# Input blocks asked for in held-back groups, fewer tables ahead of the loop, and folds at other chunks

## The chip, the cores and the metric

The kernel runs on one core of a Trainium2 chip. The metric is the device time of one execution in microseconds; a kernel's time is the median of its timed runs. One further execution is profiled, and all rows of the trace come from that one.

## What is computed

Eight sequences `x` of 6336 rows by 128 channels are convolved along the rows, channel by channel, with a filter `h` of the same length (written with Fourier transforms of twice the length). Then, for each sequence, the 128 rows with the largest scores `y @ w_gate` go through a two-layer perceptron, and its result, weighted by the sigmoid of the score, is added to them.

```
Xf = rfft(x, n=2*S, axis=1);  Hf = rfft(h, n=2*S, axis=0)
y = irfft(Xf * Hf, n=2*S, axis=1)[:, :S]
for b in range(B):
    s = y[b] @ w_gate;  top = the 128 rows of largest s
    y[b, top] += sigmoid(s[top])[:, None] * (relu(y[b, top] @ w1) @ w2)
```

## The kernel before, in words

The transform is done in two steps of matrix products, on 50 x 128 points. Work goes in **units**: unit -1 is the filter `h`, units 0 to 7 hold the input. Each unit has eight input **blocks** of 512 KB, numbered through: blocks 0 to 7 are `h`, 8 to 15 unit 0, 16 to 23 unit 1. `load_x` (L122 to L129) asks SyncE's queue for a block; `place` (L114) gives its room: the blocks up to 15 share nine rooms in turn, so that block 9 reuses block 0's room, and so on.

A block is first **folded** (`fold`, L131): an addition (L134) and a subtraction (L135) of its two halves, by VectorE or GpSimd. **Stage A** (`products_a`, L196) multiplies it with a table (`fah` for the filter, `fa` for the input), in two half-blocks t = 0 and 1 of 32 matrix instructions each. The results lie in one of three PSUM places in turn, and `leave_a` evicts them to `reg` (L211 on VectorE, L213 on ScalarE). For the filter and the first three blocks of unit 0 ScalarE evicts alone; from block 11 on VectorE takes a part or every third half-block.

Behind stage A of units -1 and 0 stands the **loop** over 13 chunks c of four frequencies ("j" in the plan): `stage_h` multiplies the filter's chunk by a table `wbuf` (L110; ScalarE L245 and L246, VectorE L253, and the spectrum is written out to `hd`), `stage_b` does the same with unit 0's chunk, VectorE multiplies it with the spectrum (L284), and GpSimd joins the parts (two operations at L289 per chunk). In the loop the blocks 16 to 23 of unit 1 are asked for, one per chunk from chunk 0 on (two there), and folded. Stage A of block 16 stands ahead of the last chunk, that of 17 to 23 behind it. Then stage C of unit 0 (L302) begins, which reads what GpSimd joined.

The program is one list of steps (`plan`), and each engine executes its part in the order in which the steps write it. What sets the order around the change:

- Before the first step the blocks 0 to 8 are asked for. Behind the second half-block of block m (m from 0 to 6) block m + 9 is asked for; it waits until TensorE has read block m.
- `fold_to(n)` emits all folds up to block n: in stage A of units -1 and 0 four blocks ahead, all on VectorE; blocks 16 to 20 and 22 on GpSimd, 21 and 23 on VectorE. In the loop it is called at chunk 0 (blocks 16, 17), and behind chunks 3, 6 and 9 (18, 19, 20); blocks 21 to 23 follow behind the last chunk.
- `ask` requests the tables of the next users, as far as six rooms reach. Behind the first half-block of blocks 9, 11 and 13 ScalarE copies one column into the next table's room (L855), and two tables are asked for; since they write the same room, SyncE can't issue them before ScalarE has written the column, and ScalarE writes it behind the evictions ahead of it. So six tables are there for the loop.
- SyncE issues its transfers in order: one that waits holds all behind it.

Of the kernel before, what the change touches and what calls it, by code (L numbers as in the profile page):

```python
# [33 lines left out]
def conv_moe(ctx, tc, x, h, w_gate, w1, w2, fa_d, wb_d, wc_d, at_d, tri_d, cst_d, outs):  # L34
    nc = tc.nc
    v = nc.vector
    g = nc.gpsimd
# [54 lines left out]
    edges = cp.tile([128, 2], F32, name="edges")  # L92
# [19 lines left out]
    blocks = {}  # L112
# [9 lines left out]
    def load_x(n):  # L122
        u, q = n // 8 - 1, n % 8
        t = place(n)
        for i in range(2 if n == 0 else 1):
            w = slice(i * 512, i * 512 + 512) if n == 0 else slice(0, 1024)
            nc.sync.dma_start(out=t[:, w], in_=h[q, :, w] if u < 0 else x[u, q])
        blocks[n] = (t[:, 0:1024].rearrange("p (d s m) -> p d s m", d=8, s=2),
                     t[:, 1024:1536].rearrange("p (d m) -> p d m", d=8))  # L129

    def fold(n, eng):  # L131
        for i in range(2 if n == 0 else 1):
            xs, es = [a[:, i * 4:i * 4 + 4] if n == 0 else a for a in blocks[n]]
            eng.tensor_tensor(out=es, in0=xs[:, :, 0], in1=xs[:, :, 1], op=ALU.add)  # L134
            eng.tensor_tensor(out=xs[:, :, 0], in0=xs[:, :, 0], in1=xs[:, :, 1], op=ALU.subtract)  # L135
# [611 lines left out]
    for u in range(NU):  # L747
        if u + 2 <= NU:
            both = merge(c_list(u), b_list(u + 1))
            n = next(i for i, s in enumerate(both) if s[0] == "b") + 2 * (u % 2)  # L750
# [17 lines left out]
    def ask(used, most=len(users)):  # L768
        while asked[0] < most:
            s = users[asked[0]]  # L770
            if s[0] == "d" and s[1] + 1 == NU:
                break
            own = [o for o in users[used:asked[0] + 1] if o[0] == "b" and o[1] >= SINGLE and o[2] % 2]
            if len(own) > 2 or s in own and s[1] > last_a[0]:
                break
            if sum(1 if o[0] == "j" else 0 if o in own else 3 if o[0] == "b" and o[1] >= SINGLE else 2
                   for o in users[used:asked[0] + 1]) > 6:
                break
            tabs[s] = (load_d if s[0] == "d" else load_b)(*s[1:])
            asked[0] += 1  # L780
# [23 lines left out]
            next(others[0], None)  # L804

    nc.sync.dma_start(out=fah, in_=fa_d[:, 1])
    for n in range(9):
        load_x(n)
    v.memset(ones16, 1.0)
    v.memset(edges[:, 0:1], -1.0)  # L810
# [2 lines left out]
    done = [1]  # L813

    def fold_to(n):
        while done[0] <= min(n, 23):
            fold(done[0], v if done[0] < 16 or done[0] in (21, 23) else g)
            done[0] += 1

    def load_constants():  # L820
# [8 lines left out]
    for s in plan:  # L829
        kind, unit = s[0], s[1]  # L830
        n = (unit + 1) * 8
        delay[0] = kind == "c" and unit + 1 == NU and not later_half and s[2] != 15
        share[0] = 5 if kind in "bc" and unit + 1 < NU or kind == "b" or delay[0] else 7
        if kind in "bdj":
            ask(used)
            used += 1
        if kind == "a":
            q, t = s[2:]
            if unit < 2 and t == 0 and (unit < 1 or q):
                fold_to(min(n + q + 4, 15) if unit < 1 else 23)  # L840
            if unit >= 2 and (q, t) == (3, 0):
                fold(n + 7, g)
            stage_a(*s[1:])
            if (q, t) == (7, 1):
                last_a[0] = unit
            if unit + 1 == NU and (q, t) == (1, 0):
                fold(n + 6, g)
            if t and n + q < 7:
                load_x(n + q + 9)
            if t and (unit, q) == (-1, 3):  # L850
                nc.sync.dma_start(out=cst, in_=cst_d)
                nc.sync.dma_start(out=fa, in_=fa_d[:, 0])
            if not t and unit == 0 and q in (1, 3, 5):
                at = used_room[0] * 512
                nc.scalar.copy(out=wbuf[:, at:at + 1], in_=edges[:, 0:1])  # L855
                ask(0, q + 1)
            if unit >= 2 and (q, t) == (1, 0):
                load_x(n + 7)
            if t:
                visit("pqx" if q in (2, 4, 7) else "x")  # L860
        elif kind == "j":
            c = s[2]
            if c == 0:
                load_x(16)
                load_x(17)
                spectra.append(stage_h(0, tabs[s][0])())
            join = stage_h(c + 1, tabs["j", -1, c + 1][0]) if c + 1 < len(KCH) else None
            n = KCH[c][1] * HD
            st = spectra.pop()
            early = c + 2 == len(KCH)  # L870
            if early:
                spectra.append(join())
            if c == 0:
                fold_to(17)
            stage_b(0, c, (tabs.pop(s)[0], [st[:, 0:n], st[:, n:2 * n]]))
            if join and not early:
                spectra.append(join())
            if 0 < c < 7:
                load_x(17 + c)
            if c == 2:  # L880
                load_constants()
            if c in (3, 6, 9):
                fold_to(17 + c // 3)
        elif kind == "b":
            stage_b(*s[1:], tabs.pop(s))
            if (unit, s[2]) == (1, 1):
                v.tensor_copy(out=upper16[0:LN], in_=upper)
                v.tensor_copy(out=ident16, in_=ident)
                v.tensor_copy(out=lanes16[:, 0:1], in_=cst[:, 0:1])
                v.tensor_scalar(out=lanes16[:, 1:2], in0=cst[:, 0:1], scalar1=-1.0, scalar2=None, op0=ALU.mult)  # L890
            if unit == SINGLE and s[2] in (9, 11):
                load_x((unit + 2) * 8 + s[2] // 2 + 1)
            visit("pqx" if s[2] % 2 or s[2] == 12 else "x")
        elif kind == "c":
            stage_c(*s[1:])
            i = HALVES.index(s[2] // 2 * 2)
            free = True
            if unit + 2 < NU and s[2] % 2:
                m = (unit + 3) * 8
                last = unit + 3 == NU  # L900
                for q in ((0,), () if last else (5,), (1,) if last else (6, 1), (4,), (2, 3), (), (), ())[i]:
                    load_x(m + q)
                q = (None, 0, None, None, 1, 4, 2, (3, 5))[i] if last else (None, 0, 5, 6, 1, 4, 2, 3)[i]
                free = i < 6
                for q in (q if isinstance(q, tuple) else () if q is None else (q,)):
                    fold(m + q, g if free or q == 5 else v)
            if unit + 1 == NU:
                for k in range(2):
                    if loaded[0] < 1:
                        load_w(loaded[0])  # L910
                        loaded[0] += 1
                if s[2] not in (4, 12):
                    visit("pq", False)
                    visit("vlx")
                if not later_half:
                    if count[0] < 4:
                        fetch()
                else:
                    if s[2] not in (0, 2, 8, 11):
                        more()  # L920
                    if s[2]:
                        visit(of=(strands,))
            else:
                visit(("vlx" if free else "x") if s[2] % 2 else "x")
        elif kind == "d":
            busy[0] = unit + 1 == NU
            stage_d(*s[1:], tabs.pop(s))
            i = s[2]
            if unit + 2 < NU:
                visit("x" if i % 2 or i == 6 else "vlx")  # L930
            elif unit + 1 == NU:
                hold[0] = i > 0
                visit(of=(strands, others) if i == 4 else None)
        elif kind == "end":
            if unit >= SINGLE:
                strands.append(search([unit], False))
                if unit + 1 == NU:
                    visit(of=(strands,))
            flush()
            busy[0] = False  # L940
            if unit == SINGLE:
                later_half.append(1)
                serial[0] = True
                while loaded[0] < 6:
                    load_w(loaded[0])
                    loaded[0] += 1
                others.append(experts())
                for i in range(8):
                    tabs["d", NU - 1, i] = load_d(NU - 1, i)
            if unit < SINGLE and unit % 2:  # L950
                strands.append(search([unit - 1, unit], True))
                if len(strands) == 1:
                    visit("x", False)
# [104 lines left out]
```

## Time and profile before

| | us |
|---|---|
| median of 3 timed runs | 779.13 |
| lowest and highest | 778.33, 780.61 |
| the profiled execution | 785.05 |
| its span, first to last instruction | 783.3 |
| TensorE busy in the span | 732.8 |
| VectorE, GpSimd, ScalarE busy | 628.5, 552.6, 450.3 |

The profiled execution is 5.92 us longer than the median of the timed ones, and its time lies 1.75 us above its span. Stage A of units -1 and 0 ends at 42.37 us of the span, the loop's last chunk and stage A of unit 1 lie between about 85 and 103 us. In a row of the trace, PE is TensorE's matrix products, PEld its weight loads, DVE VectorE, ACT ScalarE, POOL GpSimd, SPq SyncE's queue; L196 is line 196 of the kernel; "<-" behind an idle time names what ended it, and "issue" is time in which an engine waited for nothing that the profile shows.

### The profile page before, as it was taken

Reading aid. Unit: us, or ns where it says so; the run is one execution under the profiler, and the core shown is the slowest. Engines: PE = TensorE matmul, PEld = TensorE weight load, DVE = VectorE, ACT = ScalarE, POOL = GpSimd, SP = SyncE. Lnnn points to the kernel's source line nnn. Section 1 sums busy time; section 2 is a strip of 40 time slices with the busy share of each in tenths; the row PEclk is TensorE's granted clock in tenths of the full one; section 3 lists DMA queues with packets and bytes.
Section 4 is the critical chain, followed back from the end, with each engine's and each line's share of the span. In section 5 each row is a group of like instructions: output and inputs, shape, how many; then the busy total and the mean of one; then the engine's idle time right before and its main releaser. Section 6 shows DMA issues by size and latency. Waiting matters only on the chain.

```text
span 783.3 us, 39717 instructions
## 1 busy us (share of the span) xinstructions
PE 732.8 (94%) x17566; PEld 630.7 (81%) x17566; DVE 628.5 (80%) x1072; ACT 450.3 (57%) x966; POOL 552.6 (71%) x407
## 2 busy tenths in 40 slices
PE   6799999999999999999999999999999998879585
PEld 6766778888889888888898879878898888868475
DVE  6579956866676799999877999998878988965982
ACT  5687744465346566666365566655565666655561
POOL 0058939976997599859967798768995667533743
PEclk9999999999999999999999999999999999999879
DMA  8559547477856775678557765799579636541400
GB/s 325 174 196 335 207 144 252 147 212 238 278 162 208 236 260 190 184 232 270 191 170 231 261 215 162 207 349 306 167 205 319 212 106 183 146 162 30 151 12 14
DMA packets 82292, 157.64 MB, mean 201 GB/s; under 512 B 9366, under 2 KB 30088, under 8 KB 82120
## 3 DMA queue, kind: packets, MB, share of 16 engines
q1 hardware_dynamic: 81224, 154.05, 61.1%
q8 instruction: 138, 2.26, 1.2%
q0 software_dynamic: 896, 1.05, 0.5%
q14 instruction: 34, 0.28, 0.1%
HBM read 121.77 MB, written 33.29 MB: 198 GB/s over the span
## 4 chain that ended last, share of the span: by engine, by line
PE 70%; DVE 15%; issue 5%; DMA 4%; POOL 2%; SPq 1%; ACT 1%; POOLq 0%; DVEq 0%; ACTq 0%
PE pb L302 23%; PE pt L110 20%; PE pb L322 11%; PE pt L196 10%; PE pb L110 3%; PE pm L110 2%; DVE cmp L476 2%; DVE reg L278 2%; DVE tx L278 2%; DVE ss L354 1%; PE pb L196 1%; DVE st L331 1%; DVE st L332 1%; DVE num L478 1%; DMA big<-tab_wb 1%
## 5 line engine op out<-in xcount | busy, mean ns | idle before, releaser
L303 ACT COPY half<-pb 114x512 f32<-114x512 f32 x224 | 147.3, 657 | 165.3 <-PE pb L302 159.4
L338 POOL TENSOR_TENSOR tm<-st,wg 114x1024 f32<-114x1024 f32 x56 | 134.0, 2395 | 53.6 <-DVE st L332 36.4
L289 POOL TENSOR_TENSOR reg<-reg,tx 128x512 f32<-128x512 f32 (+1 forms) x104 | 130.9, 1293 | 43.5 <-PE pb L302 17.7
L289 POOL TENSOR_TENSOR big<-big,tx 128x512 f32<-128x512 f32 (+1 forms) x104 | 132.3, 1303 | 24.3 <-DVE tx L284 13.9
L302 PE MATMUL pb<-wc,reg 128*50 128x64 f32 x4096 | 125.6, 219 | 5.2 <-issue 3.5
L302 PEld LDWEIGHTS pb<-wc,reg 128*50 128x50 f32 x4096 | 120.3, 126 | 10.0 <-issue 5.6
L302 PE MATMUL pb<-wc,big 128*50 128x64 f32 x4096 | 120.7, 219 | 0.8 <-ACT reg L213 0.5
L302 PEld LDWEIGHTS pb<-wc,big 128*50 128x50 f32 x4096 | 118.4, 126 | 3.2 <-ACT reg L213 0.7
L322 PE MATMUL pb<-half,wbuf 114*50 114x128 f32 x1792 | 110.6, 273 | 2.0 <-ACT half L303 0.7
L322 PEld LDWEIGHTS pb<-half,wbuf 114*50 114x50 f32 x1792 | 96.2, 122 | 8.6 <-issue 1.3
L110 PE MATMUL pt<-big,wbuf 128*64 128x256 f32 x704 | 85.9, 388 | 0.0
L110 PE MATMUL pt<-reg,wbuf 128*64 128x256 f32 x704 | 84.9, 388 | 0.1
L284 DVE TENSOR_TENSOR tx<-pt,wbuf 128x1024 f32<-128x1024 f32 (+1 forms) x65 | 76.4, 1175 | 0.0
L213 ACT COPY reg<-pt 128x800 f32<-128x800 f32 x63 | 55.7, 936 | 33.1 <-PE pt L196 32.8
L110 PEld LDWEIGHTS pt<-big,wbuf 128*64 128x64 f32 x704 | 50.7, 135 | 23.8
L110 PEld LDWEIGHTS pt<-reg,wbuf 128*64 128x64 f32 x704 | 50.7, 135 | 22.6 <-issue 0.2
L331 DVE TENSOR_TENSOR st<-pb,st 114x512 f32<-114x512 f32 x56 | 38.6, 689 | 36.0 <-PE pb L322 22.6
L356 DVE TENSOR_REDUCE ss<-tm 114x16 f32<-114x1024 f32 x48 | 58.4, 1217 | 7.6 <-POOL tm L338 6.9
L213 ACT COPY big<-pt 128x800 f32<-128x800 f32 x56 | 49.4, 935 | 22.6 <-PE pt L196 22.5
L284 DVE TENSOR_TENSOR reg<-pt,wbuf 128x1024 f32<-128x1024 f32 (+1 forms) x39 | 45.9, 1176 | 16.6 <-PE pt L110 16.6
L196 PE MATMUL pt<-fa,big 50*64 50x100 f32 x2304 | 58.7, 249 | 0.3 <-issue 0.3
L196 PEld LDWEIGHTS pt<-fa,big 50*64 50x64 f32 x2304 | 51.3, 133 | 6.7 <-issue 4.0
(182 smaller groups left out, 1211.9 us busy)
## 6 DMA issues: line engine op xcount, KB each, us to landing
wbuf<-tab_at SPq DMA_DIRECT2D x112, 200.0 KB
out<-st SPq DMA_DIRECT2D x112, 200.0 KB
wbuf<-tab_wb SPq DMA_DIRECT2D x84, 256.0 KB
wbuf<-hd SPq DMA_DIRECT2D x84, 256.0 KB
big<-in_x SPq DMA_DIRECT2D x37, 512.0 KB
half<-in_x SPq DMA_DIRECT2D x15, 512.0 KB
hd<-st SPq DMA_DIRECT2D x24, 256.0 KB
reg<-in_x SPq DMA_DIRECT2D x12, 512.0 KB
```

Of the source, the lines that this page charges most:

```text
L110: nc.tensor.matmul(out[lo:hi], w[:, lo:hi], r, **k)
L196: nc.tensor.matmul(o, w, tab[lanes, c], start=True, stop=True)
L213: nc.scalar.copy(out=o, in_=i)
L278: v.tensor_tensor(out=o, in0=src[:, b], in1=f, op=ALU.mult)
L284: v.tensor_tensor(out=dst.rearrange("p h a j k t -> p k h a j t"), in0=src, in1=w, op=ALU.mult)
L289: g.tensor_tensor(out=yv[:, :, r], in0=yv[:, :, r], in1=zv[:, :, 1 - r], op=ALU.add if r else ALU.subtract)
L302: nc.tensor.matmul(pt[i2 * 64:i2 * 64 + N1, o:o + HD], w, wc[:, i2], start=True, stop=True)
L303: nc.scalar.copy(out=hv[0:LN, c * 4 + j:c * 4 + j + 2].rearrange("p j r m t -> p (j r) t m"), in_=pt[0:LN].rearrange("p (j t m) -> p j t m ...
L322: nc.tensor.matmul(pt[r][a * 64:a * 64 + N1, c * 128:c * 128 + 128], ats[c // 2][0:LN, c % 2, a, r], hv[0:LN, :, r, m], start=True, stop=True)
L331: v.tensor_tensor(out=st[:, 0:512], in0=pt[1][0:LN], in1=st[:, 512:1024], op=ALU.add)
L338: (v if split else g).tensor_tensor(out=tm.rearrange("p (a d) -> p a d", d=n), in0=st.rearrange("p (a d) -> p a d", d=n), in1=w.unsqueeze( ...
L356: v.tensor_reduce(out=ss[u][:, :, :, 4 * i:4 * i + 4].rearrange("p b s c -> p s c b"), in_=tm.rearrange("p (s c b d) -> p s c b d", s=2, c ...
```

## The change

Blocks 0 to 5 are asked for ahead of the first step, in place of 0 to 8. The others are asked for in four groups, each behind the first half-block of an earlier block: 6 to 8 behind block 3, 9 to 11 behind block 5, 12 and 13 behind block 7, 14 and 15 behind block 9. Ahead of each group ScalarE writes a column of its first block's room. The folds on VectorE go up to the last block asked for, and three in place of four blocks ahead in unit 0. The tables ahead of the loop are four in place of six: the column and two tables behind block 11, and the same behind block 13; the next two are asked for at the loop's first chunk, ahead of blocks 16 and 17. In the loop GpSimd folds blocks 18, 19 and 20 behind chunks 2, 4 and 6, and block 22 behind chunk 9; blocks 21 and 23 are folded by VectorE behind the last chunk, as before.

```diff
     nc.sync.dma_start(out=fah, in_=fa_d[:, 1])
-    for n in range(9):
+    for n in range(6):
         load_x(n)
...
     def fold_to(n):
         while done[0] <= min(n, 23):
-            fold(done[0], v if done[0] < 16 or done[0] in (21, 23) else g)
+            if done[0] != 22:
+                fold(done[0], g if 15 < done[0] < 21 else v)
             done[0] += 1
...
             if unit < 2 and t == 0 and (unit < 1 or q):
-                fold_to(min(n + q + 4, 15) if unit < 1 else 23)
+                fold_to(min(n + q + (4 if unit < 0 else 3), max(blocks), 15) if unit < 1 else 23)
...
-            if t and n + q < 7:
-                load_x(n + q + 9)
+            group = {3: (6, 9), 5: (9, 12), 7: (12, 14), 9: (14, 16)}.get(n + q, ())
+            if group and not t:
+                nc.scalar.copy(out=place(group[0])[:, 0:1], in_=edges[:, 0:1])
+                for m in range(*group):
+                    load_x(m)
             if t and (unit, q) == (-1, 3):
                 nc.sync.dma_start(out=cst, in_=cst_d)
                 nc.sync.dma_start(out=fa, in_=fa_d[:, 0])
-            if not t and unit == 0 and q in (1, 3, 5):
+            if not t and unit == 0 and q in (3, 5):
                 at = used_room[0] * 512
                 nc.scalar.copy(out=wbuf[:, at:at + 1], in_=edges[:, 0:1])
-                ask(0, q + 1)
+                ask(0, q - 1)
...
-            if c in (3, 6, 9):
-                fold_to(17 + c // 3)
+            if c in (2, 4, 6):
+                fold_to(17 + c // 2)
+            if c == 9:
+                fold(22, g)
```

## Rows read from the trace of the kernel before

**Rows 1.** Page: an engine's busy us, share, instructions; a queue's packets, MB, share.

```profile
PE 732.8 (94%) x17566; PEld 630.7 (81%) x17566; DVE 628.5 (80%) x1072; ACT 450.3 (57%) x966; POOL 552.6 (71%) x407
...
q8 instruction: 138, 2.26, 1.2%
```

**Rows 2.** Chain of waits, 18 to 48 us: start us, us, what.

```profile
19.12 2.29 issue
...
40.11 1.00 issue
...
42.37 2.87 PE pb L110 x24
```

**Rows 3.** Busy time by stretch: window, us, engines with records, PEclk, DMA share, GB/s.

```profile
15.90:18.87 2.97, 2.97 (x138) 2.97 (x132) 2.90 (x6) 2.69 (x5) 0.00 (x0) 1.00 1.06 412
18.87:21.41 2.54, 0.25 (x12) 0.11 (x5) 2.33 (x5) 0.94 (x2) 0.00 (x0) 1.00 0.98 358
21.41:25.21 3.80, 3.80 (x125) 3.80 (x127) 3.49 (x7) 3.06 (x5) 0.00 (x0) 0.70 0.76 270
25.21:29.90 4.69, 3.57 (x135) 3.37 (x129) 2.99 (x5) 3.84 (x7) 0.00 (x0) 0.88 0.41 126
29.90:33.58 3.68, 3.15 (x127) 3.03 (x126) 0.47 (x1) 3.09 (x6) 0.00 (x0) 1.00 0.30 77
...
37.10:41.11 4.01, 3.01 (x129) 2.89 (x128) 2.14 (x3) 1.93 (x5) 0.00 (x0) 1.00 0.57 165
...
93.28:96.91 3.63, 3.05 (x138) 2.85 (x127) 3.60 (x3) 3.63 (x8) 3.63 (x4) 1.00 0.04 11
96.91:100.57 3.66, 3.03 (x126) 2.84 (x128) 1.96 (x4) 1.80 (x4) 2.43 (x2) 1.00 0.02 4
```

**Rows 4.** DMA queues in the window 18.8 to 20.0 us.

```profile
q8 instruction: 1, 0.02, 5.6%
```

**Rows 5.** ScalarE's timeline; then SyncE's waits to 140 us (total, times, longest).

```profile
16.50 1.73 ACT L213 COPY reg<-pt 128x800 f32<-128x800 f32 x2 [0.28 <-PE pt L196]
...
31.28 0.18 ACT L855 COPY wbuf<-edges 128x1 f32<-128x1 f32 x1
...
SPq L157 <- ACT wbuf L855: 11.2, 3, 6.4
```

**Rows 6.** Timelines of VectorE and of SyncE's queue in stage A.

```profile
8.18 0.69 DVE L134 TENSOR_TENSOR half<-half 128x512 f32<-128x512 f32 x1 [2.47 <-DMA half<-in_h]
...
22.60 0.33 SPq L127 DMA_DIRECT2D half<-in_x  x1
...
24.67 0.33 SPq L127 DMA_DIRECT2D half<-in_x  x1
...
26.18 0.69 DVE L134 TENSOR_TENSOR half<-half 128x512 f32<-128x512 f32 x1 [0.28 <-DMA half<-in_x]
...
28.88 0.69 DVE L134 TENSOR_TENSOR half<-half 128x512 f32<-128x512 f32 x1 [1.21 <-DMA half<-in_x]
...
35.63 0.99 DVE L211 COPY big<-pt 128x800 f32<-128x800 f32 x1
```

**Rows 7.** GpSimd's timeline in the loop.

```profile
50.53 2.51 POOL L289 TENSOR_TENSOR big<-big,tx 128x512 f32<-128x512 f32 x2 [1.06 <-DVE tx L284]
...
61.47 2.52 POOL L289 TENSOR_TENSOR big<-big,tx 128x512 f32<-128x512 f32 x2 [1.15 <-DVE tx L284]
...
85.87 1.29 POOL L134 TENSOR_TENSOR half<-half 128x512 f32<-128x512 f32 x1
```

**Rows 8.** Busy time by stretch inside the loop, columns as in rows 3.

```profile
80.00:85.00 5.00, 5.00 (x48) 3.45 (x46) 4.79 (x7) 3.76 (x8) 4.11 (x5) 1.00 0.85 293
```

**Rows 9.** Timelines of GpSimd and TensorE behind the loop.

```profile
96.33 1.73 POOL L134 TENSOR_TENSOR half<-half 128x512 f32<-128x512 f32 x1
...
98.60 0.25 PE L196 MATMUL pt<-fa,half 50*64 50x100 f32 x1
99.47 1.57 PE L196 MATMUL pt<-fa,half 50*64 50x100 f32 x59 [0.62 <-POOL half L135]
```

## The prediction

> **What bounds the kernel now.** The page first: TensorE is busy for 94% of the span [rows 1], so a gain elsewhere counts only where TensorE stands still. The change touches only the stretch from the start to the end of the table loop and the stage A behind it, some 100 of 783 us. So the second view is the chain of waits in that stretch. After block 1 (folded from 8.18 us on [rows 6]) TensorE runs without a named wait up to the loop at 42.37, but with five pieces called "issue", the first of 2.29 us, the last of 1.00 [rows 2].
>
> What are these? TensorE executes 2 x 17566 instructions, and the queue named "instruction" moved 138 packets of together 2.26 MB [rows 1]: 35132/138 = 255 instructions and 16.4 KB each, a page. Cut at the five gaps, with cuts put between them by counting, each stretch of stage A holds 252 to 270 instruction records of both TensorE columns, those over a cut counted twice: every gap lies at the end of a page [rows 3]. The page needed at 18.87 is asked for when its forerunner begins, at 15.90; its packet shows up only in the window 18.8 to 20.0 [rows 4], with the DMA engines full (shares 1.06 and 0.98 [rows 3]), and TensorE goes on at 21.41.
>
> So stage A is **paced by the fetch of its own instructions**. From one page to the next it takes 3.63 and 3.66 us when the DMA engines are idle (share 0.04, 0.02), 3.68 and 4.01 us at shares of 0.30 and 0.57, and 5.51 us (15.90 to 21.41) when they are full; between lies 25.21 to 29.90, 4.69 us, with two single blocks in flight [rows 3]. The work of a page takes 2.97 us (15.90 to 18.87), and ScalarE's two evictions per block 0.9 us each [rows 5], 3.6 per page of two blocks. After an idle 2.5 us the granted clock is also lower for a while (0.70, 0.88), between its two levels, 1.2 and 2.4 GHz [rows 3].
>
> The Trainium skill (Runtime: NRT & Kernel Launch, section Instruction fetch mechanics) says the same of the size, 16 KiB pages of 256 instructions, but calls their cost mostly hidden; this trace differs, with up to 2.54 us at one page.
>
> **The change part by part.** The profiled execution took 785.05 us, its span 783.3; the median of the timed runs is 779.13 (778.33 to 780.61). I work out differences in the profiled execution and put them, unchanged in us, on the median. About 0.3%, 2.3 us, is what a measurement of this kernel can tell from no change.
>
> *Blocks 6 to 8 held back.* Before, nine blocks were asked for at once and land in line, one per 1.27 us (512 KB at 412 GB/s [rows 3]). Block 1 stood behind block 0's two halves only, so I take its landing as unchanged, and TensorE's work up to 15.9 us with it; a shorter queue could not help it by more than one block's 1.27 us. By the line, block 5 is there at 8.18 + 4 x 1.27 = 13.3 us. The first ScalarE column stands behind the eviction of block 3's first half, 16.50 + 0.88 [rows 5], and takes 0.18 [rows 5], so block 6 is asked for at 17.6. A block asked for with little ahead of it was folded 3.6 us (22.60 to 26.18) and 4.2 us (24.67 to 28.88) later [rows 6]: block 6 can be folded at 21.2 to 21.8, block 7 1.3 us later, block 8 another 1.3.
>
> *The same delay helps one page.* At 15.90 the DMA engines now have been idle since 13.3, so the page arrives after 3.6 us, at 19.5, in place of 21.41: 1.9 us ahead. Half of that is lost at once, since block 6's first fold (0.69 [rows 6]) ends at 21.9 to 22.5 and TensorE, done with block 5 at about 20.5 (some 1.0 us of work behind the page), waits for it; before, it came to block 6 at 22.4. Block 7 can start at 23.4 (its fold follows block 6's two operations), and the page boundary in its second half is reached at 24.2 in place of 25.21: 1.0 us ahead.
>
> *Blocks 9 to 15.* Their groups are released by the evictions of blocks 5, 7 and 9: 17.6 + 4 x 0.92 = 21.3, then about 25.7 and 29.4. So the queue is full nearly without a break until block 15 lands at about 34 to 35; before, the share fell to 0.76 and 0.41 from 21.4 us on [rows 3]. The next pages are now fetched against it. I take 5.0 us for the page from 24.2 (between 4.69 and 5.51), 4.4 for the next (between 3.68 and 4.69: the last group is still in line), 3.75 for the third (two tables only) and 4.2 for the fourth (four tables and blocks 16 and 17 in one burst; 4.01 before, with two tables and those two blocks): 29.2, 33.6, 37.35, 41.55. Before: 29.90, 33.58, 37.10, 41.11. **The lead of 1.9 us is given back page by page, and stage A ends 0.45 us later.** Bounds: all four pages at 3.6 would end at 38.6, **-2.5 us**; a start at 24.9 and 5.5, 4.7, 4.0, 4.7 would end at 43.8, **+2.7**.
>
> *What is queued behind the new waits.* SyncE stands behind each column, with cst and fa behind block 8: fa's 100 KB take 0.25 us at that rate, and block 8's first fold, 0.69 us, hides them. VectorE's folds of 14 and 15 now stand ahead of the evictions it shares from block 11 on; block 15's fold began at 28.88 and ended 1.5 us later; now it ends at about 36.5. Its eviction of block 12's first half (35.63, 0.99 us [rows 6]) moves to about 37.5; TensorE wants that bank again at block 13's second half, about 37.8 by the pages above. Covered, barely; priced in the upper bound. The columns add 4 x 0.19 and one held table column is gone: 0.6 us of ScalarE, which is idle for 0.6 to 2.1 us of each page from 21.41 on [rows 3]: nothing.
>
> *The clock.* If TensorE's waits at 20.4 and 19.1 lower it again, the page costs what that from 21.41 to 25.21 cost, 3.80 us without a gap at 0.70 [rows 3], which is less than a fetch against a full queue; inside the bounds.
>
> *Four tables in place of six, 16 and 17 behind them.* The loop needs two tables at its start, asked for at about 34.5, eight us ahead of it: hidden. Blocks 16 and 17 come some 1.3 us later; GpSimd folds them ahead of its first join, where it was idle for 1.06 us [rows 7]; the rest of the delay falls into the 1.15 us that each later chunk leaves. Cost 0.
>
> *Folds behind chunks 2, 4, 6 and 9.* GpSimd's pair of joins takes 2.52 of a chunk's 3.6 us, with 1.15 us idle; a fold takes two operations of 1.29 [rows 7]. After 2, 4 and 6 its joins run up to 2.0 us late, caught up by chunk 9, since three folds take 7.7 us and seven chunks leave 8. The slot behind chunk 9 (85.87) holds block 22's fold in place of block 20's. TensorE in the loop is busy 5.00 of every 5 us and hides it all [rows 8]. What goes is the fold of 22 behind the last join (from 96.33), for which TensorE stood still between its starts at 98.60 and 99.47, **0.87 us** [rows 9]. But the pages are late next: 93.28, 96.91, 100.57, 3.63 and 3.66 apart with the DMA engines idle [rows 3]. Without the wait, TensorE reaches the end of that page at 99.7 and stands until 100.57. **I take 0**; bounds -0.87 and 0 (above 0 needs a late GpSimd, whose joins are done by 96.33, while TensorE comes to their reader behind stage A only).
>
> Sum: +0.45 + 0 = +0.45 us; 785.5 for a profiled execution, **779.6** for the median.
>
> **Rivals.**
> *Quiet fetch, faster.* If groups of two and three leave the fetches room, all pages take 3.6: -2.5, with block 1 unchanged, 776.6. For it: the gap of 2.29 goes in any case. Against it: two single blocks already made 4.69. If the fetch cost nothing, the data and ScalarE would bound: from block 6's fold at 22.0, ten half-blocks at 0.92 and three columns end at 32.5, the ten that VectorE shares at 2.97/4 each at 39.9, against 42.37: -2.4, and with the 0.87 behind the loop -3.3: 775.8. That would be the outcome by the skill's rule (Runtime: NRT & Kernel Launch, Instruction fetch mechanics). The middle of both: **776.2**.
> *Late loads, slower.* The mechanism is the queue kept full from 18 to 35 us: each page is fetched against it, and block 15's fold, held ahead of evictions on VectorE, comes due together with the burst of four tables and two blocks. It decides from an average of 4.8 us per page on; price +2.7: **781.8**. For it: 5.51 us is on record for a full queue. Against: the last two pages meet lighter traffic.
> *The change doesn't hold.* Should the column not hold the load back, the order is much as before and the time 779.1; but such columns ahead of the tables made SyncE wait 11.2 us on ScalarE [rows 5], so they do hold.
>
> **How the numbers follow.** Forecast (a stage A within +-2.3 us) 0.60, columns that don't hold 0.02, quiet fetch 0.22, late loads 0.16. The quiet rival is over the 0.3% line at its middle, the late one too: faster 0.22, same 0.62, slower 0.16. The range reaches to the bounds, -2.5 and 0.6 of -0.87 below, +2.7 above: 776.1 to 782.0.
>
> **What would show it.** Right: the gap near 19 us falls under 1 us; TensorE waits for block 6 with about 1 us; the gaps at the next pages' ends grow to 1.5 to 2.5 us, named "issue", with the instruction packets starting 2 us or more after the page began; the loop's first product starts at 42 to 43; no wait for a GpSimd fold near 99, but an "issue" gap of 0.7 to 0.9 before 100.6. Wrong: pages of 3.6 us under a full queue, block 1 earlier than 7.5 us, or VectorE's folds of 14 and 15 named as what TensorE waited for.

## The result

| | before | changed |
|---|---|---|
| median of 14 runs, us | 779.13 | 783.86 |
| lowest and highest, us | 777.08, 781.38 | 778.44, 787.86 |
| the profiled execution, us | 785.05 | 782.47 |
| its span, us | 783.3 | 780.7 |

The ratio is 1.0053 [1.0034, 1.0073]: **the change costs 4.1 us (2.6 to 5.7)**, and the medians differ by 4.7; that is more than the 2.3 us that a measurement can tell from no change. The forecast, 779.6 and "same", was wrong; the time lies above its range (its sum gives 781.8 at the top, not 782.0; both are below), on the side of the rival called late loads.

The two profiled executions lie the other way round than the medians, before's 5.9 us above its own, the changed one's 1.4 below. The whole spans therefore can't be compared; the stretch from the start to stage C of unit 0 can. First the page of the changed kernel, beside [rows 1]:

```profile
span 780.7 us, 39723 instructions
PE 728.5 (93%) x17566; PEld 636.3 (81%) x17566; DVE 628.5 (81%) x1072; ACT 449.6 (58%) x969; POOL 551.9 (71%) x407
```

The instructions are the same but for ScalarE's, 969 in place of 966 (four columns more, one table column fewer): no work was added that could take 4 us. Next stage A cut at the ends of its instruction pages, with the columns of [rows 3], and two pages behind the loop:

```profile
14.55:17.68 3.13, 3.13 (x136) 2.91 (x128) 0.11 (x1) 3.13 (x8) 0.00 (x0) 1.00 0.19 39
17.68:23.88 6.20, 3.55 (x137) 2.99 (x127) 3.07 (x5) 4.13 (x8) 0.00 (x0) 1.00 1.02 369
23.88:28.13 4.25, 3.45 (x128) 3.03 (x127) 3.76 (x7) 3.50 (x8) 0.00 (x0) 1.00 0.85 327
28.13:32.39 4.26, 3.18 (x128) 3.02 (x127) 3.46 (x6) 3.39 (x6) 0.00 (x0) 1.00 0.76 238
32.39:37.83 5.44, 3.20 (x126) 2.82 (x126) 4.11 (x7) 2.29 (x4) 0.00 (x0) 0.93 0.67 208
37.83:43.07 5.24, 5.24 (x128) 5.24 (x131) 2.24 (x4) 1.75 (x4) 0.00 (x0) 0.50 0.49 149
43.07:44.70 1.63, 1.63 (x59) 1.50 (x52) 0.91 (x2) 0.25 (x1) 0.00 (x0) 0.73 1.07 227
...
95.77:99.41 3.64, 3.06 (x131) 2.86 (x128) 3.49 (x3) 3.64 (x8) 2.98 (x3) 1.00 0.03 10
99.41:103.33 3.92, 3.03 (x126) 2.83 (x127) 1.95 (x3) 2.37 (x4) 0.00 (x0) 1.00 0.02 4
```

The reader is to see three things. The page that ends at 17.68 ended at 21.41 before [rows 3], so the first gap named "issue" is gone and TensorE is **3.73 us ahead**: 1.35 us because this page began at 14.55 and not at 15.90, 2.38 because of the gap. The page behind it takes 6.20 us against full DMA engines (share 1.02) and hands most of that back: 23.88 stands against 25.21. TensorE stands still in it nearly as long as it did in the gap of 2.29 us, now for block 6 (start us, us, engine, line, operation, with the idle time before it and what ended it):

```profile
20.69 0.35 PE L196 MATMUL pt<-half 50*64 50x100 f32 x2 [1.92 <-DVE half L134]
```

And the last two pages take 5.44 and 5.24 us, the second of them at a granted clock of 0.50, the lower of its two levels, where before it took 4.01 at full clock [rows 3]: 43.07 stands against 41.11. The loop's first product starts at 44.77 in place of 42.37 [rows 2], **2.40 us late**, and stage C of unit 0 at 105.83 in place of 103.03: nothing was made up on the way. Stage C's line in the chain of the kernel before:

```profile
103.03 3.79 PE pb L302 x128
```

The chain of waits says what TensorE stood for (start us, us, what):

```profile
19.85 0.70 DVE half L134
...
23.43 0.45 issue
...
29.51 0.21 ACT half L851
...
29.74 4.23 DMA half<-in_x
...
34.09 0.70 DVE half L134
...
35.49 0.58 DVE big L211
...
36.68 1.15 issue
...
44.77 2.87 PE pb L110 x24
...
102.44 0.89 issue
...
105.83 3.81 PE pb L302 x128
```

Block 6's fold (19.85) stands in the chain where the first gap was. In the page from 32.39 the chain comes from the held load: ScalarE's column at 29.51, block 14 landed 4.23 us later, its fold at 34.09, an eviction on VectorE at 35.49 behind it, for which TensorE stands still for 1.09 us (35.03 to 36.12). But what ends last in that page is again a gap at its end, 1.15 us. The DMA queues in a few windows of this trace (packets, MB, share of the 16 engines) show what the gaps are. From 17.7 to 21.2 us the queue "instruction" shows no packet, and in the next window one:

```profile
q1 hardware_dynamic: 347, 1.29, 100.8%
...
q1 hardware_dynamic: 356, 0.39, 115.1%
q8 instruction: 1, 0.02, 5.2%
...
q8 instruction: 1, 0.02, 8.3%
```

The first line is 17.7 to 21.2, the next two 21.2 to 22.3, the last 100.4 to 101.4. The page begun at 17.68 asks for its follower, and that follower's packet starts 3.5 to 4.6 us later; in 32.4 to 35.3 there is none either, and one in 35.3 to 36.5. With a quiet queue it starts within 1.0 to 1.3 us: in the page begun at 99.41 nothing moves until 100.4, and the one packet of 100.4 to 101.4 starts at 100.7.

### The profile page after: what moved, and what is told of

Read it like the earlier page. It is cut to its first block, busy times and chain, and to the rows that moved or that the text cites. A ratio compares the mean times of both kernels' runs of the same rounds, so it can differ in the third digit from the quotient of the medians.

```text
span 780.7 us, 39723 instructions
## 1 busy us (share of the span) xinstructions
PE 728.5 (93%) x17566; PEld 636.3 (81%) x17566; DVE 628.5 (81%) x1072; ACT 449.6 (58%) x969; POOL 551.9 (71%) x407
## 4 chain that ended last, share of the span: by engine, by line
PE 67%; DVE 17%; DMA 6%; issue 4%; ACT 3%; SPq 1%; POOL 1%; POOLq 0%; DVEq 0%; ACTq 0%
PE pb L302 22%; PE pt L110 19%; PE pb L322 11%; PE pt L196 10%; PE pb L110 3%; DVE cmp L476 2%; DMA out<-st 2%; PE pm L110 2%; DVE tx L278 2%; DVE reg L278 2%; PE pb L196 1%; DVE ss L354 1%; DVE st L331 1%; DVE st L332 1%; ACT junk L487 1%
## 5 line engine op out<-in xcount | busy, mean ns | idle before, releaser
L110 PEld LDWEIGHTS pt<-big,wbuf 128*64 128x64 f32 x704 | 58.5, 135 | 16.6
```

The costliest lines, as they stand in the source:

```text
L110: nc.tensor.matmul(out[lo:hi], w[:, lo:hi], r, **k)
```

## Experiments

Two theories stood at the start. **Late loads on VectorE** (theory A, later L, in the expectations): blocks 14 and 15 are asked for so late that their folds hold VectorE's evictions, and TensorE waits for a PSUM place. **Fetches against bursts** (D, later F): a group of blocks issued at once stands in front of the fetch of the next instruction page; TensorE stands still, and its clock is lower behind that. Theories B and C put the loss on the tables and on the loop's folds.

### Parts of the change alone

Each kernel is the one before with one part of the diff. The kernel before ran beside them with a median of 784.19 us (30 runs; on this chip it lies 5 us above the 779.13 of the result). A ratio is the one on record for the runs of both; it is not the quotient of the two medians.

The opening alone (six blocks ahead, the four groups, the folds' look-ahead):

```diff
-    for n in range(9):
+    for n in range(6):
...
-                fold_to(min(n + q + 4, 15) if unit < 1 else 23)
+                fold_to(min(n + q + (4 if unit < 0 else 3), max(blocks), 15) if unit < 1 else 23)
...
-            if t and n + q < 7:
-                load_x(n + q + 9)
+            group = {3: (6, 9), 5: (9, 12), 7: (12, 14), 9: (14, 16)}.get(n + q, ())
...
```

> The kernel before with the opening alone changed: six blocks ahead, four groups behind ScalarE's columns, the shorter fold look-ahead; six tables and the old folds in the loop stay. Theory A (late groups: the last two groups land late, their folds stand ahead of VectorE's evictions, TensorE stalls and its clock falls for the last pages of stage A): 3 to 5 us slower than before, stage A of unit 0 ends at 43.5 to 45.5 us. Theory B (tables: the burst of four tables and two blocks at the end of stage A is what hurts): within 1 us of before. Theory C (the loop's folds): within 1 us of before.

Measured: 788.34 us, ratio 1.0062 [1.0037, 1.0088]. The whole loss, as far as the intervals tell, is in this part. Its trace has the strongest case of the second theory (stretches, columns as above):

```profile
17.67:26.91 9.24, 3.96 (x131) 3.31 (x126) 5.50 (x8) 4.06 (x7) 0.00 (x0) 0.77 0.92 337
26.91:32.04 5.13, 5.13 (x125) 5.13 (x128) 2.67 (x4) 3.26 (x7) 0.00 (x0) 0.50 0.49 174
```

The page takes 9.24 us though VectorE and ScalarE are busy for 5.50 and 4.06 of them, and the next one runs wholly at 0.50. From 17.7 to 24.5 us the instruction queue moved nothing while the blocks' queue filled all 16 engines:

```profile
q1 hardware_dynamic: 920, 2.43, 99.8%
```

The tables alone:

```diff
-            if not t and unit == 0 and q in (1, 3, 5):
+            if not t and unit == 0 and q in (3, 5):
...
-                ask(0, q + 1)
+                ask(0, q - 1)
```

> The kernel before with four tables ahead of the loop in place of six, nothing else. Theory A: within 1 us of before, stage A ends at 42 to 42.8 us. Theory B: 2 to 4 us slower, with longer pages at the end of stage A. Theory C: within 1 us.

Measured: 785.43 us, ratio 1.0012 [0.9997, 1.0028]. Nothing to be told from no change.

The folds in the loop alone:

```diff
-            fold(done[0], v if done[0] < 16 or done[0] in (21, 23) else g)
+            if done[0] != 22:
+                fold(done[0], g if 15 < done[0] < 21 else v)
...
-            if c in (3, 6, 9):
-                fold_to(17 + c // 3)
+            if c in (2, 4, 6):
+                fold_to(17 + c // 2)
+            if c == 9:
+                fold(22, g)
```

> The kernel before with the loop's folds alone changed (18, 19, 20 behind chunks 2, 4, 6, block 22 behind chunk 9). Theory A and B: 0 to 0.5 us faster; TensorE's wait for GpSimd's fold behind the loop goes, and the wait for the next page of instructions stands in its place, so stage C begins at most 0.3 us earlier. Theory C: 2 us or more slower. The plain hope (the wait of 0.87 us goes): 0.9 us faster.

Measured: 785.70 us, ratio 0.9995 [0.9972, 1.0018]. Its chain of waits shows why removing a wait of 0.87 us [rows 9] gives nothing:

```profile
95.71 0.61 issue
...
99.36 1.17 issue
...
103.02 3.00 PE pb L302 x100
```

And GpSimd's timeline behind chunk 9 (start us, us, engine, line, operation):

```profile
85.38 1.31 POOL L134 TENSOR_TENSOR half<-half 128x512 f32<-128x512 f32 x1
...
88.00 7.86 POOL L289 TENSOR_TENSOR big<-big,tx 128x512 f32<-128x512 f32 x6
```

Block 22 is folded at 85.38, no wait for GpSimd is left, and a gap of 1.17 us at a page's end stands in its place: stage C begins at 103.02, before at 103.03, though the loop's first product starts at 41.88 here and at 42.37 before. **A wait was exchanged for the next one.**

The last group early: in the changed kernel blocks 14 and 15 are asked for with 12 and 13, behind block 7.

```diff
-            group = {3: (6, 9), 5: (9, 12), 7: (12, 14), 9: (14, 16)}.get(n + q, ())
+            group = {3: (6, 9), 5: (9, 12), 7: (12, 16)}.get(n + q, ())
```

> The changed kernel with blocks 14 and 15 asked for together with 12 and 13, behind block 7, and no group behind block 9. Theory A: most of the loss comes back, 2 to 4 us faster than the changed kernel, and the third page from block 9's on takes 3.6 to 4.3 us in place of 5.44. Rival D (the queue kept full costs the instruction fetches): no better than the changed kernel, since the queue is just as full; page times stay at 4.2 to 5.4 us.

Measured: 790.84 us, ratio 1.0059 [1.0034, 1.0083]. If the late folds had set the time of the whole kernel, this would have given it back; the time gave nothing. Its pages:

```profile
18.04:25.05 7.01, 4.89 (x137) 4.53 (x133) 3.52 (x6) 3.90 (x8) 0.00 (x0) 0.74 1.00 360
25.05:29.37 4.32, 4.32 (x139) 4.32 (x134) 3.87 (x7) 3.19 (x7) 0.00 (x0) 0.62 0.67 247
29.37:34.59 5.22, 3.32 (x139) 3.04 (x131) 4.34 (x7) 4.12 (x8) 0.00 (x0) 1.00 0.81 322
34.59:38.90 4.31, 4.31 (x125) 4.31 (x128) 2.73 (x5) 1.46 (x3) 0.00 (x0) 0.60 0.39 116
```

Two pages against DMA engines at shares of 1.00 and 0.81 take 7.01 and 5.22 us, and behind each the clock is at 0.62 and 0.60 for the next. The first theory is not refuted by this run: the last page above, the one that took 5.44 us in the changed kernel, takes 4.31 without standing still, and the loop begins earlier than at the 44.77 of the changed kernel:

```profile
43.24 2.86 PE pb L110 x23
```

That is 0.87 us behind the kernel before, of 5.8 us by which this trace's span is longer (789.1 against 783.3); where the rest arises is open.

### The opening by itself

A difference of 3 us is easier seen in a short kernel. The next ones stop ahead of stage C of unit 0, so they hold the stretch in question and little else; eight small writes stand in for the output.

```diff
+        if kind == "c":
+            break
...
+    for u in range(NU):
+        nc.sync.dma_start(out=outs[u][0, :, :, 0:4], in_=reg[1][0:N1, 0:1024]...)
```

Single executions of such a kernel lie up to 5 us apart, so the medians and means here are over all of them, and the figures behind a plus-minus are 95% bounds of a difference of means (1.96 standard errors, which is a little narrow for so few runs).

> The kernel before cut off behind stage A of unit 1: the opening, the loop and that stage alone, and eight small writes; the rest is left out. It is the base for the three others. By the trace of the whole kernel stage C would begin at 103 us, so some 105 to 112 us in all; its runs should lie closer together than those of the whole kernel, within 3 us.

> The changed kernel cut off in the same way. If the whole loss of 4 to 5 us is made ahead of stage C, it is 4 to 5 us over the cut kernel before; if only what the two profiles show, 2.4 to 2.8 us; if the loss is made later, under 1 us.

Measured: 110.19 and 112.84 us. The pair was run a second time:

> The cut kernel before once more, as the base on the chip of the next three: 109.5 to 111 us.

> The cut changed kernel on the same chip: 2 to 3.3 us over the cut kernel before, as in the first pair (2.65).

Measured: 110.22 and 112.57 us. Together, 13 runs each: 110.22 and 112.71, means 110.45 and 112.99, a difference of **2.5 +- 1.0 us**. The changed opening also scatters more: the lowest runs lie 0.8 us apart (109.53 and 110.31), the highest 3.5 (111.96 and 115.47). So the opening's loss is there without the rest of the kernel. It is less than the 4.1 us of the whole kernel, but the two intervals overlap (1.6 to 3.5, 2.6 to 5.7); whether something is lost behind stage C too is not settled.

*Traffic added.* The cut kernel before, all blocks as early as before, and six transfers of 2.25 MB in all behind block 15, into rooms that nobody reads:

```diff
                 load_x(n + q + 9)
+                if n + q == 6:
+                    for i in range(3):
+                        nc.sync.dma_start(out=xr[i][:, 0:1024], in_=x[3, i])
+                        nc.sync.dma_start(out=xr[i][:, 1024:1536], in_=x[3, i + 3][:, 0:512])
```

> The cut kernel before with six transfers more (2.25 MB, read by nobody) behind block 15 in SyncE's queue: every block is as early as before, and the DMA engines stay full some 5.7 us longer, to about 34 us. Theory F (pages of instructions are fetched behind a full queue of blocks, TensorE stands still, and its clock falls after it): 1.5 to 3 us slower than the cut kernel before, the pages from 25 and 30 us on at 4.3 to 5.5 us. Theory L (late blocks: their folds hold TensorE and VectorE's evictions): within 0.5 us of it.

Measured: 114.19 us, 3.5 +- 0.7 above the base. Here no fold is late, and TensorE still loses more than the change does:

```profile
25.16:30.05 4.89, 3.42 (x140) 3.26 (x134) 3.41 (x5) 3.81 (x7) 0.00 (x0) 0.94 0.81 270
30.05:36.18 6.13, 3.15 (x129) 3.02 (x128) 0.00 (x0) 3.34 (x6) 0.00 (x0) 0.98 0.89 344
36.18:41.30 5.12, 5.12 (x125) 5.12 (x128) 1.57 (x2) 1.63 (x4) 0.00 (x0) 0.50 0.35 114
```

The piece of its chain that ends the second stretch:

```profile
33.18 2.98 issue
```

In the second stretch VectorE does nothing (0.00, x0), so it can't be what TensorE waits for; the page stands 2.98 us at its end, and the next runs at 0.50 throughout. **A full queue alone can make such a loss.** It does not show that the whole loss of the change is made so.

*The first group given back.* The changed opening with blocks 0 to 8 ahead as before, and only three groups, behind blocks 5, 7 and 9:

```diff
-    for n in range(6):
+    for n in range(9):
...
-            group = {3: (6, 9), 5: (9, 12), 7: (12, 14), 9: (14, 16)}.get(n + q, ())
+            group = {5: (9, 12), 7: (12, 14), 9: (14, 16)}.get(n + q, ())
```

> The cut changed kernel with blocks 0 to 8 asked for ahead as before, and groups 9 to 11, 12 and 13, 14 and 15 behind blocks 5, 7 and 9. If the first held group (6 to 8) makes the loss, by its late blocks and by the page that is fetched behind it, 2 to 4 us come back against the cut changed kernel. If the last groups make it, by their folds ahead of VectorE's evictions or by a queue that is full from 25 to 34 us, it stays within 1 us of the cut changed kernel.

Measured: 112.23 us (108.92 to 114.06), 0.5 below the changed opening's median, the means 1.0 +- 1.6 apart: not told from no difference. The first burst is not the one cause; in the trace the next takes its place:

```profile
23.75:30.31 6.56, 3.56 (x130) 3.00 (x129) 2.77 (x4) 3.41 (x7) 0.00 (x0) 0.87 0.91 295
30.31:35.43 5.12, 5.12 (x125) 5.12 (x128) 3.96 (x6) 2.98 (x6) 0.00 (x0) 0.50 0.56 195
```

*The bursts made light.* Blocks 9 to 15 are read with 128 of their 1024 columns, an eighth of the bytes, in the changed opening and in the one before; the waits and the order stay.

```diff
-            w = slice(i * 512, i * 512 + 512) if n == 0 else slice(0, 1024)
+            w = slice(i * 512, i * 512 + 512) if n == 0 else slice(0, 128 if 8 < n < 16 else 1024)
...
```

> The cut changed kernel, where blocks 9 to 15 are loaded with 128 of their 1024 columns only (the rest of their rooms holds what was there): waits and order as in the changed kernel, the DMA engines nearly idle from about 22 us on. Theory F (pages of instructions fetched behind bursts of blocks): pages from 24 us on take 3.5 to 3.9 us, the clock stays up from there, 2.5 to 4.5 us faster than the cut changed kernel (0.138 to 0.141 of the whole kernel before, where the cut changed one had 0.1443). Theory L (what counts is that the columns are written late, so that blocks are asked for late): at most 1.5 us faster.

> The cut kernel before with the same light loads of blocks 9 to 15. Theory F: 1 to 3 us faster than the cut kernel before, since its gaps near 19 and 29 us come from the queue too; the gain is smaller than that of the changed kernel, which has the queue full for longer. If the light loads gain the same in both, the change's loss does not come from the queue.

Measured: 109.49 and 108.36 us. The difference is 1.3 +- 1.1 where it was 2.5 +- 1.0; that it fell is not clear of these bounds. What is left of it seems to lie at the group that is still heavy, blocks 6 to 8, in the changed one's trace:

```profile
18.69:25.90 7.21, 5.47 (x129) 4.71 (x128) 5.15 (x8) 4.09 (x7) 0.00 (x0) 0.68 0.65 241
25.90:31.02 5.12, 5.12 (x125) 5.12 (x128) 4.08 (x7) 3.29 (x7) 0.00 (x0) 0.50 0.12 32
```

So that group was made light too: blocks 6 to 15 with 128 columns, three rooms cleared by GpSimd ahead of the first step.

```diff
-            w = slice(i * 512, i * 512 + 512) if n == 0 else slice(0, 1024)
+            w = slice(i * 512, i * 512 + 512) if n == 0 else slice(0, 128 if 5 < n < 16 else 1024)
...
+    g.memset(half[:, 0:4608], 0.0)
```

> The cut changed kernel with blocks 6 to 15 all loaded with 128 of 1024 columns (three rooms are cleared by GpSimd first). With light loads of 9 to 15 alone the page from 18.7 us on still took 7.2 us. If the bursts make that page long (its fetch waits 4 to 5 us behind blocks 6 to 8, which themselves take 3.6 us to land): 5 us or less, no wait over 1 us there, the clock at most 3.4 us at half, and 3.5 to 5 us faster than the cut changed kernel. If the hold behind ScalarE's column makes it: 6 us or more, and at most 3 us faster.

Measured: 105.84 us, 6.6 +- 1.2 below the changed opening. The held loads, their columns and their folds are all there, in the same order:

```profile
18.25:23.07 4.82, 3.55 (x129) 3.00 (x128) 4.12 (x7) 4.06 (x7) 0.00 (x0) 1.00 0.33 81
23.07:26.65 3.58, 3.14 (x129) 2.92 (x128) 3.27 (x6) 3.16 (x7) 0.00 (x0) 1.00 0.15 40
26.65:30.36 3.71, 3.18 (x130) 3.03 (x129) 3.31 (x6) 3.44 (x7) 0.00 (x0) 1.00 0.16 45
30.36:33.90 3.54, 2.96 (x129) 2.81 (x128) 3.39 (x6) 2.59 (x5) 0.00 (x0) 1.00 0.29 82
33.90:37.63 3.73, 3.27 (x131) 2.96 (x130) 2.75 (x4) 1.90 (x4) 0.00 (x0) 1.00 0.51 155
```

At shares of 0.15 to 0.51 the pages take 3.54 to 3.73 us, and the clock stays at 1.00. **With the waits in place and the bytes gone, the long pages and the low clock are gone too.** One page of 4.82 us is left; in it TensorE stands still for 0.28 us for block 6's fold and for 0.95 us at the page's end. What the waits cost by themselves is not measured: the kernel before was not run with blocks 6 to 15 light.

*The late folds taken off VectorE.* In the changed opening GpSimd folds blocks 14 and 15.

```diff
-                fold(done[0], g if 15 < done[0] < 21 else v)
+                fold(done[0], g if 13 < done[0] < 21 else v)
```

> The cut changed kernel with blocks 14 and 15 folded by GpSimd, which is idle there, so that no late fold stands ahead of VectorE's evictions. Theory L: 1 to 2.5 us faster than the cut changed kernel. Theory F: within 0.7 us of it, and the pages after 32 us still end with a wait for instructions.

Measured: 112.99 us. The changed opening had not run on that chip, so both were run on one chip:

> The cut changed kernel with blocks 14 and 15 folded by GpSimd, now on the chip of its base. If the late folds ahead of VectorE's evictions make the long page from 33 us on (5.44, 5.24 and 4.90 us in three traces, 4.08 in the one with these folds moved): 0.8 to 1.3 us faster than the cut changed kernel. If the fetches alone make it: within 0.4 us of it.

Measured: 111.28 us, against 112.57 for the changed opening beside it. All runs of both together are 0.8 +- 1.1 below the changed opening: what the late folds cost is at most some 2 us and may be nothing (on the one chip alone 1.5 +- 1.7). The page of these folds without them on VectorE, first in the second run's trace (two lines), then in the first run's:

```profile
33.18:38.35 5.17, 2.96 (x128) 2.79 (x128) 1.99 (x3) 2.30 (x4) 3.91 (x4) 0.96 0.74 222
38.35:43.47 5.12, 5.12 (x125) 5.12 (x128) 1.67 (x3) 1.64 (x4) 1.15 (x1) 0.50 0.49 136
...
33.63:37.70 4.07, 2.97 (x126) 2.78 (x126) 2.10 (x3) 2.31 (x5) 2.93 (x3) 1.00 0.81 239
```

The same kernel shows 5.17 us and the low clock behind it in one execution, 4.07 us at full clock in the other, so a long page doesn't need the late folds. That they cost nothing doesn't follow. In the changed kernel the fetch ends last in this page, but in the traces of t2_after, t10_after and e1_opening an eviction behind block 15's fold holds TensorE for another 0.61, 0.76 and 0.69 us after the next page has come; in t10_after:

```profile
41.78 2.90 PE L196 MATMUL pt<-fa,half 50*64 50x100 f32 x64 [0.76 <-DVE big L211]
```

*A version meant to be faster.* If bursts are the harm, one might ask for all early. Blocks 9 to 11 get rooms of their own and are asked for at the start, 12 blocks in a line; 12 to 15 follow as rooms come free.

```diff
-    for n in range(9):
+    for n in range(12):
...
-            if t and n + q < 7:
-                load_x(n + q + 9)
+            if t and n + q < 4:
+                load_x(n + q + 12)
```

> The cut kernel before with rooms of their own for blocks 9, 10 and 11, which are asked for at the start; 12 to 15 take the rooms of 0 to 3. The blocks stream without a break and the last lands at about 26 us in place of 28.8, so the DMA engines are quiet from there. Theory F: the page from 25 us on takes 3.6 in place of 4.7 us, 0.5 to 1.5 us faster than the cut kernel before; the page near 19 us stays late. Theory L: no change, the blocks were not late before.

Measured: 111.63 us, 1.6 +- 0.9 above the base. The gain of 0.5 to 1.5 us that the second theory expected did not come. That it is slower is not shown, since it ran on another chip than the base, one on which the whole kernel before took 787.64 us (778.96 and 785.32 beside the two runs of the base). The trace has two long pages, the first against a full queue:

```profile
15.77:22.49 6.72, 3.06 (x129) 2.92 (x129) 6.55 (x11) 3.32 (x5) 0.00 (x0) 1.00 1.03 408
22.49:28.24 5.75, 4.62 (x128) 4.41 (x128) 5.33 (x9) 3.55 (x5) 0.00 (x0) 0.70 0.43 160
```

No version that loads all the bytes was found to beat the kernel before.

## Why the prediction was wrong, step by step

**The mechanism was right.** Stage A is paced by the fetch of its instructions; the gap named "issue" near 19 us went; block 6 was folded at 19.85, 3.65 us after ScalarE's column let SyncE ask for it at 16.20, inside the 3.6 to 4.2 of the sum, and TensorE waited for it, for 1.92 us and not for about 1; the gaps named "issue" stand at the pages' ends. The rival at 775.8 took the fetch to cost nothing; in the runs it costs least where little else is in flight: with light blocks the pages from 23.07 us on take 3.54 to 3.73 us, 0.44 to 0.58 of them standing still, and pages that met a burst took 4.07 to 9.24. The Trainium skill (Runtime: NRT & Kernel Launch, section Instruction fetch mechanics) calls the cost of crossing to the next page mostly hidden; these traces differ, by those 0.44 to 0.58 us of a page at the least.

**Tables and loop folds: right.** 0 and 0 within the intervals, by the two runs of these parts alone; behind the loop the gap at 102.44 (0.89 us) stands where the wait of 0.87 us for the fold was [rows 9], as the prediction had it from the pages' spacing. From the loop's first product to stage C the traces show 60.66 us before, 61.06 in the changed kernel and 61.14 with the folds alone: nothing gained there.

**The first page: too careful.** 19.5 was forecast, 17.68 came. TensorE reached its start at 14.55, not at 15.90, a point that the prediction had held fixed, and the page took 3.13 us without a gap. Between 14 and 16 us it executed 103 products, before 56, busy 2.00 of the 2.00 us and at a granted clock of 1.00 both times; why is not shown. This lead was worth nothing, since block 6 and the fetch behind its group decide next.

**The page with block 6: mis-sized.** 4.7 us (19.5 to 24.2) was forecast; it took 6.20 in the changed kernel, 9.24 with the opening alone, 7.01 with the larger last group. In the changed kernel's own trace its end, 23.88, is near the 24.2 of the sum, because the lead was larger; in the others it is not (26.91, 25.05). The sum reckoned this fetch as one of a steady full queue. The one on record started 2.97 us after its page began (15.90 to 18.87); behind a group just issued they started 3.65 us after it in the changed kernel, 4.0 to 4.9 in four others, 6.4 in t10_after and 6.9 with the opening alone. The upper bound of 5.5 for a page, from the one trace of [rows 3], was no bound even for the kernel before: its cut version in the second run (t9_before), with no group, had a page of 6.44 us, whose fetch started 4.1 us after it began:

```profile
15.76:22.20 6.44, 3.05 (x128) 2.91 (x128) 6.03 (x10) 3.34 (x5) 0.00 (x0) 1.00 1.00 390
```

**The third and fourth pages: mis-sized, and decisive in this trace.** 3.75 and 4.2 us were forecast, 5.44 and 5.24 came, 2.7 us more together, against a lead of 1.2 at 32.39 (33.6 was forecast). The third was taken as light, "two tables only"; but blocks 14 and 15, asked for at 29.7, were in flight in it (share 0.67), and its fetch started 2.9 us or more after the page began, when 1.0 to 1.3 is the quiet case. The late folds that the prediction called "covered, barely" are in the chain here and held TensorE for 1.09 us of this page; the runs without them on VectorE have it at 5.17 and 4.07.

**The clock: not "inside the bounds".** The prediction let the clock fall in at most one page, for less than the fetch takes. Taking each stretch's length by twice what its granted clock lacks of 1.00 gives the time at the lower level: before 3.80 x 0.60 + 4.69 x 0.24 = 3.4 us [rows 3]; changed 5.44 x 0.14 + 5.24 + 1.63 x 0.54 = 6.9; with the opening alone 9.24 x 0.46 + 5.13 = 9.4 and a little in the next. In these traces the fall lies in or behind a page in which TensorE stood still (5.44 less 3.20 busy in the changed kernel, 2.54 less 0.25 before, 9.24 less 3.96 with the opening alone). At the lower level the page itself takes 5.12 to 5.24 us, longer than most fetches here: the stall is paid, then the slow page. It would have cost one term more in the sum, a page of 5.1 us in place of 3.7, behind a long stall. On the last line of the sum stage A was to end 0.45 us later; in the trace it ends 1.96 later (43.07 against 41.11) and stage C begins 2.80 later. The rest of the 4.1 us lies outside this stretch or in the scatter of single executions; its cause stays open.

**The rival.** "Late loads, slower" named the right side and, in its first half, the right cause: pages fetched against a full queue. The four pages from 23.88 to 43.07 averaged the 4.8 us that it asked for. Its price, +2.7 at stage A's end, is near the 2.4 of the trace and the 2.5 of the cut pair; its second half, the late folds, is not shown as a cost of the whole and not excluded. It got 0.16, because 5.51 us was taken as the worst a page can cost, and because the last two pages were thought to meet lighter traffic. Both reasons fell.

## What to carry to other kernels

Where the chain shows "issue" gaps after equal counts of instructions, look for the fetch of instructions among the transfers: in these runs it started later when the DMA engines were full. Here loads asked for one by one, as rooms came free, did better than loads held back and released in groups. A wait removed from such a stretch is worth only what the next page's arrival leaves of it, so list the pages' ends first and price the wait between them. A long stall of TensorE can cost twice, as the stall and as the slower page that the granted clock shows behind it.

## What the runs showed of the hardware

- The fetch of a page of 255 instructions (16.4 KB) started 1.0 to 1.3 us after the page ahead of it began where little else was in flight and a gap's end shows that beginning, 2.5 to 4.2 in a queue that had long been full (2.5 and 3.8 with the added traffic, 2.97 in the whole kernel before, 4.1 in t9_before, 4.2 with twelve blocks asked for at the start), and 3.65 to 6.9 behind a group of blocks just issued. Its packet is small beside that: 5.2% of the 16 engines' time in a window of 1.1 us. The ranges overlap; whether a fresh group holds it longer than a full queue was not settled.
- The first block of 512 KB of a group of three, asked for with the queue empty, could be folded 3.65 us later (16.20 to 19.85), where a full line delivers one per 1.27 us (512 KB at the 412 GB/s of [rows 3]).
- The clock did not fall behind each stall: the page from 17.68 to 23.88 had TensorE idle for 2.65 us in three pieces (1.92, 0.28 and 0.45) and kept 1.00, the page from 32.39 in the same trace 2.24 us in two (1.09 and 1.15), and the next ran at 0.50. In the light kernel, with 0.4 to 0.6 us idle per page from 23.07 on, it never fell in stage A.
